# Attention with mixed heads, then two MoE layers, on one core: first loads on two DMA queues, the first block's scores moved in two halves, and a new layout of all steps

## The chip, the core and the metric

The kernel runs on one core of one Trainium2 chip. The core has five engines that run side by side, each working through its own instructions in order: TensorE (PE, whose weight loads are listed as PEld), VectorE (DVE), ScalarE (ACT), GpSimd (POOL) and SyncE (SP). SP computes nothing here; it issues the DMA transfers, which 16 DMA engines carry out. The metric is the device time of one execution in microseconds, as the median of several runs.

## What is computed

The reference has three stages, one after the other. The attention mixes the heads twice, before and after the softmax, so all 12 heads of a query are needed together.

```
scores = scale * q @ k^T                       # 4 batches, 12 heads, 448 queries, 448 keys, 64 wide
scores = einsum('bhij,hg->bgij', scores, w_pre)
attn   = exp(scores - max); attn /= sum + 1e-9
attn   = einsum('bhij,hg->bgij', attn, w_post)
x      = attn @ v                              # then (1792 tokens, 768)
x      = (s * relu(x @ w_in)**2 + b) @ w_out   # 768 -> 2048 -> 768
h      = x @ w_in2
out    = (h * cos(h)) @ w_out2
```

The second layer's weights arrive as float64 and are split on the chip into pairs of float32 parts. Most products are taken as a high and a low part (`qh`, `ql`; `wh`, `wl`; `gh`, `gl`) for precision.

## The kernel before

**Blocks and tiles.** The queries are cut into 16 blocks (`n`), four to a batch, of 120, 110, 110 and 110 queries. A block is worked on in tiles of R = 10 queries with all 12 heads, so that a tile has 120 rows and 448 columns; there are 180 tiles, and the first block has 12 of them. In this text they are counted from 0, so block 1 begins with tile 12 and block 4 with tile 45.

**Scores of a block.** `keys` and `queries` load and transpose k and q on PE (tiles `tk`, `tq`) and split them on ACT (`ks`, `qh`) and DVE (`ks`, `ql`). `scores` makes the product of one head with two matmuls (`sps`), copies it out on ACT or DVE (tile `s`; for block 0 a piece of the tile `at`), and then a DMA moves it into the block's tile `m`, where rows are ordered by query and head. This move (`m<-s`, in block 0 `m<-at`) is how the heads of one query come together. There are N_S = 4 buffers `s`, so a fifth copy waits until the move of the first has landed. There are two tiles `m`, so block n takes the one of block n-2.

**Work of a tile.** `shi` takes the high part of a tile's rows of `m` (tile `mh`, on ACT or POOL, line 421 or 423), POOL subtracts it (426), PE mixes the heads with three matmuls (tile `p`, 431 to 433), DVE takes the maximum (442), ACT the exponential with its sum (449), DVE makes the weights of a pair of tiles from the sums (`st`, 456 and 458; `w`, 462), PE mixes again and transposes (tile `a`, 471), and ACT or DVE keeps the result (`at`, 483 or 485). When two blocks are through, PE multiplies with v in three groups (`vps`, 506), the results are copied (`xo`) and stored to memory as `x`.

**The layers.** `mlp` loads x back, splits it (727), turns weights into pairs (673 to 701), and runs `hidden` (751) and `output` (814 and 842) for each of 16 weight pieces and four token groups.

**What sets the order.** No order is written out. Each step is given to a planner (class `Plan`) with a position, the engine or engines that may do it, a cost in ns, the steps it waits for, and the buffers that it takes and frees. The planner replays time with these costs: each time an engine is free, it gives it the ready step with the lowest position. It knows a fixed handover between engines (`SYNC`), a rate of transfers (`wire`), and the buffers' counts. The instructions are then written down in the order of that replay. On the chip the engines keep this order and wait by semaphores. So a cost in the planner moves nothing by itself, but it can change which step stands before which, and which of two engines gets a step. The constants `STEP`, `OFF`, `W1`, `W2`, `TOK` and the like only set positions. All transfers stand on SP's queue.

## Time and profile before

| | |
|---|---|
| median of three runs | 1465.22 us (1461.92 to 1465.97) |
| the profiled execution, its own time | 1466.36 us |
| its span, from first to last instruction | 1464.4 us, so 2.0 us lie around it |
| PE busy | 1411.6 us, 96% |
| DVE, ACT, POOL busy | 1202.2, 766.5, 622.2 us |
| mean granted clock of TensorE | 0.984 |

A share of busy time says how often an engine has something in it, over stages that differ: here the attention up to about 520 us, then the layers. What an engine waits for in a stretch is read from the idle time ahead of an instruction and the engine that ended it. The granted clock is given as a share of the full level (2.4 GHz); 0.5 is the lower level (1.2 GHz).

### The profile page before, as it was taken

The page shows a single profiled execution, that of the slowest core. Times are in us where ns is not written, and L with a number is a line of the kernel's source. Part 1 is how long each engine was busy: PE and PEld are TensorE (multiplying, and loading weights), DVE is VectorE, ACT ScalarE, POOL GpSimd, SP SyncE. Part 2 cuts the span into 40 slices and gives each one's busy share as a digit, 9 for nine tenths or more (in the row PEclk, how much of TensorE's full clock was granted, in tenths as well). Part 3 has the DMA queues.
Part 4 walks back from the last instruction along what each step waited for, and adds up shares of the span by engine and source line. Part 5 has one row for each costly group of instructions (what it writes and reads, how often), then busy time and mean ns, then how long its engine had stood idle before and what let it go on. Part 6 is the DMA issues. An engine that isn't in the chain of part 4 may idle for free.

```text
span 1464.4 us, 23087 instructions
## 1 busy us (share of the span) xinstructions
PE 1411.6 (96%) x8220; PEld 1228.8 (84%) x8220; DVE 1202.2 (82%) x2195; ACT 766.5 (52%) x1605; POOL 622.2 (42%) x554
## 2 busy tenths in 40 slices
PE   5898999999999799999999999999999999999998
PEld 4787888887888677888888888888999898998998
DVE  4687788677877779888987878798898999999975
ACT  4676676666767655433322332356655455454442
POOL 0554564445545535333432432424544454544431
PEclk8899999999999999999999999999999999999999
DMA  6645374464454352221212112111211211211103
GB/s 162 145 133 140 112 168 131 130 153 119 126 145 132 104 170 79 71 65 55 66 54 65 46 63 65 44 33 44 65 55 44 65 55 44 66 44 60 59 33 119
DMA packets 159485, 129.20 MB, mean 88 GB/s; under 512 B 93867, under 2 KB 147083, under 8 KB 159371
## 3 DMA queue, kind: packets, MB, share of 16 engines
q1 hardware_dynamic: 159371, 127.73, 31.0%
q8 instruction: 65, 1.06, 0.3%
q14 instruction: 49, 0.40, 0.1%
...
## 4 chain that ended last, share of the span: by engine, by line
PE 85%; DMA 6%; DVE 5%; ACT 2%; POOL 1%; issue 1%; SPq 1%; DVEq 0%; POOLq 0%; ACTq 0%
PE h L751 30%; PE o L842 16%; PE o L814 15%; PE a L471 8%; PE vps L506 5%; PE sps L357 4%; DMA m<-s 2%; PE p L431 2%; PE p L433 2%; PE p L432 2%; DMA qn<-in_q_dram 1%; PE tq L326 1%; DVE st L442 1%; DMA m<-x 1%; SPq L222 1%
## 5 line engine op out<-in xcount | busy, mean ns | idle before, releaser
L699 POOL TENSOR_TENSOR cm<-ca,wh 128x384 f32<-128x384 f32 x128 | 158.4, 1239 | 382.8 <-ACT wh L693 378.4
L426 POOL TENSOR_TENSOR m<-m,mh 120x448 fp32r<-120x448 f32 x180 | 208.2, 1162 | 189.0 <-ACT mh L421 176.1
L751 PE MATMUL h<-m,wh 128*128 128x512 f32 x672 | 215.7, 390 | 0.0
L471 PEld LDWEIGHTS a<-w,e 120*112 120x112 f32 x1440 | 172.8, 182 | 32.7 <-issue 13.4
L471 PE MATMUL a<-w,e 120*112 120x120 f32 x1440 | 181.5, 274 | 15.2 <-DVE w L462 14.7
L751 PE MATMUL h<-x,wh 128*128 128x256 f32 (+1 forms) x768 | 190.1, 338 | 1.1 <-DVE x L727 1.0
L701 POOL TENSOR_TENSOR wl<-cm,ce 128x384 fp32r<-128x384 f32 x128 | 148.3, 1160 | 83.2 <-DVE ce L697 79.2
L751 PE MATMUL h<-m,wl 128*128 128x512 f32 x384 | 150.3, 391 | 0.0
L751 PEld LDWEIGHTS h<-x,wh 128*128 128x128 f32 x768 | 131.7, 188 | 18.1 <-DVE x L727 2.3
L751 PEld LDWEIGHTS h<-m,wh 128*128 128x128 f32 x672 | 125.2, 188 | 25.6 <-issue 0.7
L814 PE MATMUL o<-gh,wl 128*128 128x512 f32 (+1 forms) x384 | 139.7, 364 | 0.8 <-POOL wl L701 0.8
L814 PE MATMUL o<-gl,wh 128*128 128x512 f32 (+1 forms) x384 | 139.6, 364 | 0.0
L814 PE MATMUL o<-gh,wh 128*128 128x512 f32 (+1 forms) x384 | 139.3, 363 | 0.0
L449 ACT ACTIVATE e<-p,st 120x448 f32<-120x448 f32 x180 | 114.1, 634 | 37.0 <-DVE st L442 34.6
L751 PE MATMUL h<-x,wl 128*128 128x512 f32 (+1 forms) x384 | 129.8, 338 | 0.0
L442 DVE TENSOR_REDUCE st<-p 120x1 f32<-120x448 f32 x180 | 109.9, 615 | 16.6 <-PE p L433 15.8
L791 POOL TENSOR_TENSOR tb<-ta,tb 128x512 f32<-128x512 f32 (+1 forms) x64 | 80.4, 1257 | 101.2 <-ACT tb L789 95.9
L842 PE MATMUL o<-wh,gl 128*128 128x384 f32 x448 | 114.0, 335 | 0.0
L842 PE MATMUL o<-wl,gh 128*128 128x384 f32 x448 | 113.9, 335 | 0.0
L842 PE MATMUL o<-wh,gh 128*128 128x384 f32 x448 | 113.8, 334 | 0.0
L675 DVE SCALAR_TENSOR_TENSOR cm<-cm,raw 128x384 f32<-128x384 f32 x128 | 95.7, 748 | 20.2 <-ACT cm L673 20.1
L851 DVE TENSOR_TENSOR acc<-acc,o 128x384 f32<-128x384 f32 x196 | 101.0, 544 | 13.1 <-PE o L842 13.0
...
## 6 DMA issues: line engine op xcount, KB each, us to landing
m<-s SPq DMA_DIRECT2D x144, 192.5 KB
raw<-in_moe_w_in_dram SPq DMA_DIRECT2D x64, 384.0 KB
raw<-in_moe_w_out_dram SPq DMA_DIRECT2D x64, 384.0 KB
...
m<-s SPq DMA_DIRECT2D x36, 210.0 KB
...
out_dram<-acc SPq DMA_DIRECT2D x14, 384.0 KB
...
```

The costliest lines, as they stand in the source:

```text
L426: a2 = pl.add(p - OFF[1] * STEP, "pool", 1110, lambda hh=hh, src=src: nc.gpsimd.tensor_tensor(out=src(), in0=src().bitcast(F32), in1=hh.ti ...
L442: nc.vector.tensor_reduce(out=hst.tile[:, 0, z:z + 1], in_=hp.tile, axis=AX, op=ALU.max, negate=True)
L449: nc.scalar.activation(out=he.tile, in_=hp.tile, func=AF.Exp, bias=hst.tile[:, 0, z:z + 1], accum_out=hst.tile[:, 1, z:z + 1])
L471: nc.tensor.matmul(out=ha.tile[:, c * L:(c + 1) * L], lhsT=he.tile[:, c * CH:(c + 1) * CH], rhs=hw2.tile[:, z], start=True, stop=True)
L675: a = pl.add(p0 + dp, "dve", 470, lambda hm=hm, high=high: nc.vector.scalar_tensor_tensor(out=hm.tile, in0=hm.tile, scalar=2.0 ** -15, in1 ...
L699: a = pl.add(p0 + 6 * dp, "pool", 1050, lambda hm=hm, ha=ha, flat=flat: nc.gpsimd.tensor_tensor(out=hm.tile, in0=ha.tile.bitcast(F32), in1 ...
L701: got.append(pl.add(p0 + 7 * dp, "pool", 1050, lambda hm=hm, he=he, flat=flat: nc.gpsimd.tensor_tensor(out=flat(1), in0=hm.tile, in1=he.ti ...
L751: nc.tensor.matmul(out=hp.tile, lhsT=w, rhs=cols(z_, j, k)[:, 0], start=(k == 0 and y == 0), stop=(k == KD - 1 and y == 2))
L791: a = pl.add(p + 7 * dp, "pool", n * 2.4 + 100, lambda h1=h1, h2=h2: nc.gpsimd.tensor_tensor(out=h2.tile, in0=h1.tile, in1=h2.tile, op=ALU ...
L814: nc.tensor.matmul(out=hp.tile, lhsT=w, rhs=x, start=(c == 0 and y == 0), stop=(c == 1 and y == 2))
L842: nc.tensor.matmul(out=hp[e].tile, lhsT=x, rhs=w[:, e * HD:(e + 1) * HD], start=(c == 0 and y == 0), stop=(c == 1 and y == 2))
L851: got.append(pl.add(p, "dve", 470, lambda e=e, hp=hp, view=view: nc.vector.tensor_tensor(out=view(), in0=view(), in1=hp[e].tile, op=ALU.ad ...
```

## The change

The first loads (k and q of block 0, the mask and the two mixing matrices) and the first half of each head's move in block 0 may now stand on SP's queue or on ACT's; the planner chooses. The three constants' loads get a low position (`CST`), so they come early. Block 0 loads each q once and not twice; POOL makes the second copy on the chip. In block 0 each head's move into `m` is split in two (`SUB`): queries 0 to 59 first, 60 to 119 with a higher position (`SECOND`), and a tile waits only for the half that it lies in. In block 0's keys the high part may be taken by DVE too. The planner gets other numbers: a handover for each engine, a dearer PE before 26 us (`COLD`), other costs of steps and of issues, a lower rate of transfers. All position constants are new. No instruction of the steady part is of a new kind.

```diff
-    SYNC = 130.0
+    SYNC = dict(pe=210.0, act=150.0, dve=130.0, pool=90.0, sp=130.0, none=130.0)
+    COLD = 26000.0
...
+                    elif e == "pe" and t < self.COLD:
+                        end = t + 1.8 * s["engs"][e]
...
-                        wire = max(end + 650.0, wire) + s["nbytes"] / 360.0
+                        wire = max(end + 650.0, wire) + s["nbytes"] / s["rate"]
...
-STEP = 2427.2
+STEP = 2364.9
...
+        if two:
+            return pl.add(pos, ("sp", "act"), (cost, cost), lambda e: (nc.sync if e == "sp" else nc.scalar).dma_start(out=out(), in_=in_()), after, take, use, nbytes=nbytes, behind=behind)
...
+    SUB = [2 if n == 0 else 1 for n in range(NBLK)]
...
-            e = pl.add(p + 500 + 100 * z, "act", 430.0, lambda z=z: hi(z), [a])
...
+            e = pl.add(p + 500 + 100 * z, ("act", "dve"), (480.0, 580.0), lambda e, z=z: hi(z, e), [a]) if not b else pl.add(p + 500 + 100 * z, "act", 480.0, lambda z=z: hi(z, "act"), [a])
...
-        for i in range(2):
...
+        for i in range(2 if n else 1):
...
+        if not n:
+            d.append(pl.add(p - 1000, "pool", 340.0, lambda: nc.gpsimd.tensor_scalar(out=raw()[:, :, 1], in0=raw()[:, :, 0], scalar1=1.0, scalar2=0.0, op0=ALU.mult, op1=ALU.add), d))
...
-            m_done.setdefault(n, []).append(dma(p + QZ * z + 1000, place, held, rows * S * 4, [e], use=[hs], behind=m_done.get(n, [])[:1]))
+            rs = rows // SUB[n]
+            for u in range(SUB[n]):
...
+                    return hm.tile.bitcast(F32).rearrange("(r h) t j -> r h t j", h=H)[:, h, u * rs // R:(u + 1) * rs // R]
...
+                    d = dma(p + u * SECOND, place, lambda: held()[u * rs:(u + 1) * rs], rs * S * 4, [e], use=[hs],
+                            behind=m_done.get(n, [])[:1] + (m_sub[n, 0] if u else []), cost=870.0, two=SUB[n] > 1 and u == 0)
...
-        a1 = pl.add(p - OFF[0] * STEP, e, (540.0, 480.0)[:len(e)], shi if len(e) > 1 else lambda shi=shi: shi("pool"), m_done[n], take=[hh])
+        a1 = pl.add(p - OFF[0] * STEP, e, (540.0, 480.0)[:len(e)], shi if len(e) > 1 else lambda shi=shi: shi("pool"), m_sub[n, t["t"] // (BLOCKS[n % 4][1] // R // SUB[n])], take=[hh])
...
-OFF = (4.214, 4.426, 3.27, 2.518, 2.539, 1.825)
-AVP = (2.733, 2696.6)
+OFF = (3.52, 4.361, 3.326, 2.518, 1.368, 2.311)
+AVP = (1.516, 1918.9)
...
+SECOND = 9999.326
+CST = -2999.464
...
-W1 = (-1.242, 4.431)
-W2 = (-1.044, 7.344)
+W1 = (-2.306, 4.548)
+W2 = (-3.818, 7.382)
```

The order of the instructions shows what becomes of this. On SP's queue, at the start of the program, these are the transfers of block 0 before (`at<-in_k` and `at<-in_q` are the loads, `m<-at` the moves of its scores, `qn` the queries of block 1, `w` the mixing matrices):

```order
L222 DMA ident<-in_cst_dram 128x128
L222 DMA at<-in_k_dram 112x4x64 x4
L222 DMA at<-in_q_dram 120x4x64 x2
L222 DMA at<-in_k_dram 112x4x64 x4
L222 DMA at<-in_q_dram 120x4x64 x2
L222 DMA at<-in_k_dram 112x4x64 x4
L222 DMA at<-in_q_dram 120x4x64 x2
L222 DMA m<-at 10x12x448 x4
L222 DMA mask<-in_cst_dram 120x10
L222 DMA m<-at 10x12x448 x3
L222 DMA qn<-in_q_dram 110x4x64 x2
L222 DMA w_110<-in_w_pre_dram 120x1x12
```

After these stand `w_post`, five more `m<-at`, four `qn` and four `m<-s`. Then come, before the last four `m<-s` of block 1, six more loads of q and v, four `m<-s`, two loads of v and four of the next batch's k. The same queue of the changed kernel:

```order
L228 DMA ident<-in_cst_dram 128x128
L227 DMA at<-in_k_dram 112x4x64 x3
L227 DMA at<-in_q_dram 120x4x64
L227 DMA at<-in_k_dram 112x4x64
L227 DMA w_110<-in_w_post_dram 120x1x12
L227 DMA at<-in_k_dram 112x4x64 x2
L227 DMA at<-in_q_dram 120x4x64
L227 DMA m<-at 10x6x448 x7
L228 DMA qn<-in_q_dram 110x4x64 x4
L228 DMA m<-at 10x6x448 x3
L228 DMA qn<-in_q_dram 110x4x64 x2
L228 DMA m<-at 10x6x448 x9
```

SP now has 9 loads ahead of the first move instead of 18 (both besides `ident`), 19 half moves instead of 12 whole ones, and after them the 12 moves of block 1 with only five loads of q between them; loads of v and of the next k come later.

On ACT's queue, at the start of the program, the changed kernel has this (before, ACT begins with the table load and issues nothing):

```order
L227 DMA mask<-in_cst_dram 120x10
L227 DMA at<-in_k_dram 112x4x64 x4
L227 DMA w_110<-in_w_pre_dram 120x1x12
L227 DMA at<-in_k_dram 112x4x64
L227 DMA at<-in_q_dram 120x4x64
L227 DMA at<-in_k_dram 112x4x64
L306 ACT_TABLE_LOAD
L306 ACTIVATE ks<-tk 64x448 x4
L343 ACTIVATE qh<-tq 128x480
L306 ACTIVATE ks<-tk 64x448 x4
L378 ACTIVATE at<-sps 120x448 x2
L227 DMA m<-at 10x6x448
```

Nine issues now stand ahead of the table load, and further on four more half moves each stand between two copies of scores.

On DVE, in the stretch in which the scores of block 4 are made (tiles 37 to 41 before), its copies `s<-sps` stand like this among the work of the tiles before the change:

```order
L368 COPY s<-sps 120x448 x2
L456 TENSOR_SCALAR st<-st 120x2
L442 TENSOR_REDUCE st<-p 120x1
L458 RECIPROCAL st<-st 120x2
L462 TENSOR_TENSOR w_1521<-wq,st 120x240
L333 TENSOR_TENSOR ql<-tq,qh 128x480
L302 TENSOR_TENSOR ks<-tk,ks 64x448 x2
L368 COPY s<-sps 120x448
L442 TENSOR_REDUCE st<-p 120x1
L368 COPY s<-sps 120x448
L456 TENSOR_SCALAR st<-st 120x2
L368 COPY s<-sps 120x448
```

and in the changed kernel:

```order
L380 COPY s<-sps 120x448
L345 TENSOR_TENSOR ql<-tq,qh 128x480
L312 TENSOR_TENSOR ks<-tk,ks 64x448 x2
L467 TENSOR_REDUCE st<-p 120x1 x2
L481 TENSOR_SCALAR st<-st 120x2
L510 COPY at<-a 112x48x10
L483 RECIPROCAL st<-st 120x2
L487 TENSOR_TENSOR w_1493<-wq,st 120x240
L312 TENSOR_TENSOR ks<-tk,ks 64x448 x2
L345 TENSOR_TENSOR ql<-tq,qh 128x480
L467 TENSOR_REDUCE st<-p 120x1 x2
L481 TENSOR_SCALAR st<-st 120x2
```

Five copies have become one. Over the whole program DVE's copies of scores go from 66 to 48 and ACT's from 114 to 132; DVE's copies `xo` from 42 to 2 and ACT's from 6 to 49 (rows of the order, where one row may be one half of a result); ACT's `mh` from 130 to 105 and POOL's from 50 to 75. On PE the 12 products of block 4 stood between the mixing of tiles 36 and 41, and now stand between those of tiles 34 and 41; blocks 6, 8, 10, 12 and 14 move in the same way. The three groups `vps` of blocks 12 and 13 move too: the last of them stood behind the mixing of tile 168 and now stands behind that of tile 166; no more of them follow until all tiles are mixed.

## Rows read from the trace of the kernel before

**Rows 1.** Windows of whole stages: us, busy of each engine, granted clock, DMA share

```profile
80.00:480.00 400.00, 384.04 (x2830) 327.84 (x2829) 305.73 (x627) 276.23 (x652) 198.29 (x194) 0.98 0.51 135
480.00:525.00 45.00, 34.74 (x257) 28.43 (x258) 38.29 (x75) 29.98 (x68) 22.50 (x18) 0.92 0.37 123
565.00:1452.00 887.00, 887.00 (x4584) 784.86 (x4583) 776.08 (x1345) 393.94 (x743) 356.98 (x301) 1.00 0.19 56
```

**Rows 2.** Timeline of SP's queue, the first 28 us: start, length, transfer

```profile
8.92 2.56 SPq L222 DMA_DIRECT2D at<-in_k_dram  x4
11.53 1.14 SPq L222 DMA_DIRECT2D at<-in_q_dram  x2
...
21.92 0.82 SPq L222 DMA_DIRECT2D w<-in_w_pre_dram  x1
...
23.69 4.25 SPq L222 DMA_DIRECT2D m<-at  x5
```

**Rows 3.** Windows of 10 us, the last three columns: granted clock, DMA share, GB/s

```profile
10.00:20.00 10.00, 8.50 (x37) 6.83 (x37) 7.36 (x12) 7.63 (x15) 0.00 (x0) 1.00 0.66 173
40.00:50.00 10.00, 9.95 (x68) 8.84 (x66) 8.68 (x20) 7.15 (x19) 6.83 (x7) 1.00 0.92 186
```

**Rows 4.** Timeline of ACT and POOL, start of the program to the first tile

```profile
0.73 1.28 ACT L298 ACT_TABLE_LOAD   x1 [0.73 <-PEq L904]
6.06 1.09 ACT L298 ACTIVATE ks<-tk 64x448 fp32r<-64x448 f32 x2 [4.04 <-PE tk L289]
...
23.76 0.54 ACT L366 ACTIVATE at<-sps 120x448 f32<-120x448 f32 x1 [0.83 <-PE sps L357]
33.04 0.58 ACT L421 ACTIVATE mh<-m 120x448 fp32r<-120x448 f32 x1 [1.15 <-DMA qn<-in_q_dram]
33.14 0.56 POOL L423 TENSOR_SCALAR mh<-m 120x448 fp32r<-120x448 f32 x1 [32.70 <-DMA qn<-in_q_dram]
```

**Rows 5.** Timeline of SP's queue, 46 to 58 us

```profile
47.92 6.25 SPq L222 DMA_DIRECT2D rk<-in_k_dram  x4
54.29 3.46 SPq L222 DMA_DIRECT2D m<-s  x4
```

**Rows 6.** Timeline of PE: first product of tile 12, and two later waits

```profile
62.85 0.46 PE L431 MATMUL p<-mh,wp_h 120*120 120x448 f32 x1 [2.06 <-ACT mh L421]
76.96 1.04 PE L471 MATMUL a<-w,e 120*112 120x120 f32 x8 [0.40 <-DVE w L462]
143.78 1.05 PE L471 MATMUL a<-w,e 120*112 120x120 f32 x8 [3.03 <-DVE w L462]
```

**Rows 7.** PE's waits, 64 to 480 us: total us, times, longest

```profile
PE a L471 <- DVE w L462: 10.1, 8, 3.0
PE p L431 <- ACT e L449: 4.0, 8, 1.1
```

**Rows 8.** Timelines of DVE and of ACT, 142 to 144 us

```profile
142.10 0.62 DVE L368 COPY s<-sps 120x448 f32<-120x448 f32 x1 [1.70 <-DMA m<-s]
143.29 0.54 ACT L366 ACTIVATE s<-sps 120x448 f32<-120x448 f32 x1 [4.14 <-DMA m<-s]
```

**Rows 9.** Windows behind three of the waits, columns as in rows 1

```profile
145.00:148.00 3.00, 2.96 (x13) 2.52 (x12) 1.91 (x6) 1.88 (x5) 0.47 (x1) 0.54 0.53 165
265.00:271.00 6.00, 5.66 (x25) 5.46 (x26) 3.39 (x9) 3.83 (x10) 1.13 (x1) 0.50 0.50 139
388.00:391.00 3.00, 3.00 (x14) 2.76 (x13) 1.69 (x5) 2.52 (x7) 2.27 (x2) 0.50 0.48 151
```

**Rows 10.** The end of the attention: a PE wait, and the window behind it

```profile
491.24 0.70 PE L431 MATMUL p<-mh,wp_h 120*120 120x448 f32 x1 [3.97 <-ACT e L449]
497.00:517.00 20.00, 14.79 (x105) 12.58 (x104) 19.11 (x36) 14.81 (x36) 12.77 (x10) 1.00 0.31 104
```

**Rows 11.** All waits of the program: ACT and DVE for a free `s`

```profile
ACT s L366 <- DMA m<-s: 17.6, 13, 4.1
DVE s L368 <- DMA m<-s: 11.4, 15, 1.7
```

More of the change, by code (lines that the diff above doesn't have):

```diff
@@ L52, in hold, with add @@
         return Hold(ring)
-    def add(self, pos, eng, cost, fn, after=(), take=(), use=(), lag=0.0, behind=(), nbytes=0, port=False):
+    def add(self, pos, eng, cost, fn, after=(), take=(), use=(), lag=0.0, behind=(), nbytes=0, port=False, rate=200.0):
         n = len(self.steps)
@@ L63, in add @@
         self.steps.append(dict(id=n, pos=pos, engs=dict(zip(engs, costs)), fn=fn, after=[a for a in after if a is not None],
-                               take=take, use=use, lag=lag, behind=list(behind), nbytes=nbytes, port=port))
+                               take=take, use=use, lag=lag, behind=list(behind), nbytes=nbytes, port=port, rate=rate))
         return n
@@ L219, in attention, with dma @@
         pl.ring(name, cap, name != "ps")
-    def dma(pos, out, in_, nbytes, after=(), take=(), use=(), behind=()):
-        return pl.add(pos, "sp", 515.0 if not use else 700.0, lambda: nc.sync.dma_start(out=out(), in_=in_()), after, take, use, nbytes=nbytes, behind=behind)
+    def dma(pos, out, in_, nbytes, after=(), take=(), use=(), behind=(), cost=650.0, two=False):
+        if two:
+            return pl.add(pos, ("sp", "act"), (cost, cost), lambda e: (nc.sync if e == "sp" else nc.scalar).dma_start(out=out(), in_=in_()), after, take, use, nbytes=nbytes, behind=behind)
+        return pl.add(pos, "sp", cost, lambda: nc.sync.dma_start(out=out(), in_=in_()), after, take, use, nbytes=nbytes, behind=behind)
     tiles, first = [], []
+    SUB = [2 if n == 0 else 1 for n in range(NBLK)]
     for n in range(NBLK):
@@ L240, in attention @@
     wq = one.tile([L, H, R], F32, name="wq")
-    d_id = dma(-5200, lambda: ident, lambda: cst[:, 0:128], 65536)
-    d_mk = dma(5000, lambda: mask, lambda: cst[0:L, 128:128 + R], 4800)
-    d_w = [dma(5000, lambda i=i: w12[:, i], lambda w=w: w.rearrange("(o h) g -> o h g", o=1).to_broadcast([R, H, H]), 5760) for i, w in enumerate((w_pre, w_post))]
+    d_id = dma(-5200, lambda: ident, lambda: cst[:, 0:128], 65536, cost=450.0)
+    d_mk = dma(CST, lambda: mask, lambda: cst[0:L, 128:128 + R], 4800, two=True)
+    d_w = [dma(CST, lambda i=i: w12[:, i], lambda w=w: w.rearrange("(o h) g -> o h g", o=1).to_broadcast([R, H, H]), 5760, cost=950.0, two=True) for i, w in enumerate((w_pre, w_post))]
     hw = pl.hold("e")
@@ L261, in attention @@
     KW = 8 * D
[L262 removed]
+    mh, m_first, m_done, m_sub, later = {}, {}, {}, {}, []
     m_all = m_p.tile([128, 2, 12 * S], F32R, name="m")
@@ L281, in keys @@
             d.append(dma(p - 6000, lambda h=h: load(h), lambda h=h: k[b, 2 * g + h].rearrange("(p z) d -> p z d", z=4), CH * KW * 2,
-                         take=[hr] if b and h == 0 else [], behind=d if h else m_done[0][-1:] if b else [s_open]))
+                         take=[hr] if b and h == 0 else [], behind=d if h else m_done[0][-1:] if b else [s_open], two=not b))
         bank, ring, tag = (ps_s, "ps", "s") if b else (ps_a, "pa", "a") if g % 2 else (ps_p, "pp", "p")
@@ L318, in queries @@
         d = []
-        for i in range(2):
-            d.append(dma(p - 8000 if n else p - 5500, lambda i=i: load(i), lambda: q[b, 4 * g:4 * g + 4, i0:i0 + rows, :].rearrange("h i d -> i h d"), rows * 2048,
-                         take=[hr] if n and i == 0 else [], behind=d if i else m_done[0][5:6] if n else [s_open]))
+        for i in range(2 if n else 1):
+            d.append(dma(p - 8000 if n else p - 5500, lambda i=i: load(i), lambda: q[b, 4 * g:4 * g + 4, i0:i0 + rows, :].rearrange("h i d -> i h d"), rows * 1024,
+                         take=[hr] if n and i == 0 else [], behind=d if i else m_done[0][-1:] if n else [s_open], two=not n, cost=600.0))
+        if not n:
+            d.append(pl.add(p - 1000, "pool", 340.0, lambda: nc.gpsimd.tensor_scalar(out=raw()[:, :, 1], in0=raw()[:, :, 0], scalar1=1.0, scalar2=0.0, op0=ALU.mult, op1=ALU.add), d))
         def trans():
@@ L381, in attention @@
         scores(0, g, PRO[0] * g + PRO[2])
+    for move in later:
+        move()
     for n in range(1, NBLK):
@@ L507, in prod, with evac @@
                                              start=(c == 0), stop=(c == 3), tile_position=(0, 64 * y))
-            a = pl.add(p + AVP[1] * 2 * pp, "pe", 2 * AVC - 150, prod, kept[b, hf] + [d for c in range(4) for d in v_done[b, c]],
+            a = pl.add(p + AVP[1] * 2 * pp, "pe", 3300.0, prod, kept[b, hf] + [d for c in range(4) for d in v_done[b, c]],
                        take=[hp], use=[hb] + [vh[b, c] for c in range(4)])
-            def evac(e, hp=hp, ho=ho, blocks=blocks, base=base, wid=wid):
+            def evac(e, hp=hp, ho=ho, blocks=[(i0 + u * rows // SUB[4 * b + 2 * hf + z], rows // SUB[4 * b + 2 * hf + z]) for z, (i0, rows) in enumerate(blocks)
+                                              for u in range(SUB[4 * b + 2 * hf + z])], base=base, wid=wid):
                 ho.tile = xo_p.tile([128, 2 * width[0]], F32, tag="xo", name="xo")[:, :2 * wid].rearrange("p (g n) -> p g n", g=2)
@@ L627, in dma @@
     def dma(pos, out, in_, nbytes, after=(), take=(), use=(), behind=()):
-        return pl.add(pos, "sp", 515.0 if not use else 700.0, lambda: nc.sync.dma_start(out=out(), in_=in_()), after, take, use, nbytes=nbytes, behind=behind)
+        return pl.add(pos, "sp", 450.0, lambda: nc.sync.dma_start(out=out(), in_=in_()), after, take, use, nbytes=nbytes, behind=behind, rate=300.0)
     c_sb = [dma(t_start - 15000, lambda i=i: P["sc"][:, i:i + 1], lambda a=a: a.rearrange("(a o) -> a o", a=1).to_broadcast([128, 1]), 512, [g_right]) for i, a in enumerate((s, b))]
```

51 lines of the change are left out of this document (30 added, 21 removed).

## The prediction

> **What bounds the kernel now.** First I read the windows of whole stages [rows 1]. From 565 to 1452 us PE is busy for all of 887 us at the full clock: the layers are bound by PE. The change leaves the number of PE's matmuls as it is, so this stretch should keep its length, whatever the new positions do to DVE or POOL there. What can be won lies before 565 us. From 80 to 480 us PE is idle for 400 - 384.0 = 16.0 us and runs at a mean of 0.98 of the clock; from 480 to 525 us it is idle for 10.3 us; the rest is in the first 65 us.
>
> Then I read the start in order of time. SP issues the 18 loads of k and q without a gap until 12.67 us, at 2.56/4 = 0.64 us for a k and 1.14/2 = 0.57 us for a q [rows 2]. The DMA engines are then busy for 0.66 of the time, while later they reach 0.92 [rows 3]. So the first loads are held by the issuing queue, not by the engines. The last score of block 0 is copied by 23.76 + 0.54 = 24.30 us [rows 4]; but SP spends 21.92 to 23.69 us on the two mixing matrices and then 4.25 us on the last five moves, until 27.94 us [rows 2]. The first tile's `mh` starts at 33.04 us [rows 4], 5.10 us behind the end of that last issue. POOL had been idle for 32.70 us. Tile 12, the first of block 1, is mixed at 62.85 us after another wait of 2.06 us [rows 6]: between block 1's moves SP issued four loads of the next k for 6.25 us, and its last four moves only from 54.29 to 57.75 us [rows 5].
>
> Last the middle. PE's waits from 64 to 480 us sum to 14 us, 10.1 of them for the weights `w` from DVE and 4.0 for the exponential [rows 7]. Neither engine is short of time there (DVE 305.7, ACT 276.2 of 400 us) [rows 1]. At 143.78 us PE waits for 3.03 us [rows 6], and just before, DVE stood 1.70 us and ACT 4.14 us in front of a copy into `s` whose buffer was still being moved [rows 8]. An engine works in order, so maximum, weights and exponential stood behind that copy. This is block 4, whose 12 scores stand within five tiles. Block 2, whose 12 stand within eight, shows a wait of 0.40 us [rows 6]. In all, ACT waits 17.6 us and DVE 11.4 us for a free `s` [rows 11].
>
> **The change part by part.** I cost it against the profiled execution: 1464.4 us of span and 2.0 around it, 1466.36 us. The median of the runs is 1465.22, 1.1 us less.
>
> *Start.* On two queues SP has 9 loads and `ident`, ACT nine. By the rows SP needs 6 x 0.64 + 2 x 0.57 + 0.8 + 0.4 = 6.2 us and is free near 7 us instead of 12.7. What an issue costs on ACT no row shows; I take SP's, which gives 6 x 0.64 + 0.57 + 0.8 + about 0.5 = 5.7 us, so ACT ends near 6.4 us and, since the table load of 1.28 us now stands behind, can begin at 7.7 instead of 6.06 us [rows 4]. That loss is partly covered by DVE, which takes the first key. Nothing covers the rest: until the last score ACT has 9 + 3 + 8 + 1 activations at about 0.54 us and five half moves. A half move has no row; its ends are 0.43 us (half of 4.25/5 = 0.85) and 0.85 us, and I take 0.85, the row of the same transfer, because the loads show no saving with size either (0.64 for 112 KB, 0.57 for 120 KB). So ACT needs 11.3 + 4.3 = 15.6 us and ends near 23.3 us: the last copy is hardly earlier than 24.30. The gain comes behind it: no matrices and no row of five whole moves are left, the last half is issued by about 24.2 us instead of 27.9, and lands 5.1 us later at most and 2.6 us (half the bytes) at least. The first `mh` then starts at 27 to 29 us, 4 to 6 us earlier.
>
> POOL's three copies of q are bounded by nothing below and by 0.56 us each above (the row of 448 columns [rows 4]; these have 256); POOL is idle there, but each lies between its q and the transpose. They replace three loads of 0.57 us and 120 KB.
>
> Tile 12 checks this from SP's side: from 24.4 us on SP still has, until the last move of block 1, six q (3.4 us), 12 second halves (10.2), 12 moves of block 1 (10.2) and five q (2.9), and ends at 51.1 us instead of 57.75. With halves at 0.43 it would be 46, and PE's own work would then be what ends last. **Start: -6 us, bounds -2 to -9.** What is late next is the second half of block 0 (tile 6), with PE doing `a` and block 1's scores meanwhile.
>
> *Middle.* Blocks 4, 6, 8, 10, 12 and 14 now spread their scores over seven tiles, and of block 4's 12 copies DVE keeps one where it had five between the same weights. If all six cost what block 2 does, 14.1 - 6 x 0.4 = 11.7 us of waits go. With them go the stretches at the lower level (1.2 GHz) that followed three of the waits, 12 us in which PE was busy for 11.6 [rows 9]; at the higher level half of that would do, 5.8 us. What speaks against taking it all: the copies that leave DVE go to ACT, where the exponential stands behind them. I take half of 17.5. **Middle: -9 us, bounds 0 to -17.**
>
> *End of the attention.* PE waits 3.97 us at 491 us, and DVE is busy for 19.1 of 20 us behind that [rows 10]. By the order, DVE's steps for the layers among the last 13 tiles fall from about 16 to 8; the rest comes after, beside 3.1 us of `a` and three `vps`. Against this, the last `vps` that could fill a gap now comes two tiles earlier. **End: -2 us, bounds -7 to +4.**
>
> *Layers.* **0**: PE is the bound, and the steps that moved lie beside it [rows 1].
>
> Sum: 1466.36 - 6 - 9 - 2 = 1449.4, or 1448.2 against the median; I say 1449.
>
> **Rivals.**
>
> *Only the start gains.* The waits of the middle move from DVE to ACT and stay as long. For it: 17.6 of the 29.0 us of waits for `s` are ACT's already [rows 11]. Against: eight tiles instead of five did away with them in block 2. Time 1465.2 - 6 = 1459, at most 1461.
>
> *Two queues bring nothing at the start.* The same DMA engines carry both queues; if these set the pace, issuing earlier only makes the transfers queue. 1,704 KB of loads and 1,260 KB of half moves (by the shapes in the order, 4 bytes each) at the 186 GB/s of the busiest row take 16 us [rows 3], less than the 24 us that the copies need, so the row speaks against it; block 1's moves could still meet it. Then only the middle and the end are left: 1465.2 - 11 = 1454. The Trainium skill's page "DMA: Bandwidth & Descriptors", section "Issuing engines are not separate DMA queues", says so for the general case: issuing from several engines saves only the sequencer's time to initiate, since all run on the same 16 DMA engines; by that rule alone the start would give nothing. The trace agrees with half of it: here it is the sequencer's time that is short, with the engines at 0.66.
>
> *Slower: ACT blocks.* ACT now makes nearly all copies of `s` in the even blocks, and each waits for a move; the exponential of the next tile stands behind it, then `w`, then `a` on PE. If all 29.0 us that ACT and DVE wait now came together on ACT and reached PE, the middle would lose 29.0 - 14.1 = 15 us more: 1465.2 - 6 + 15 = 1474. It decides from the point where more than 14.1 + 6 = 20 us of such waits reach PE. Against: with seven tiles a copy has half as much again of the time it had.
>
> *Nothing to measure.* The parts cancel: a start of -2 and a middle of 0: 1463.
>
> **How the numbers follow.** The forecast (1442 to 1457) 0.57, only the start 0.17, two queues without gain 0.08, ACT blocks 0.10, nothing 0.08. A change of 0.3% (4.4 us) is about what a measurement of this kernel can tell from none. Faster: 0.57 + 0.08 + 0.13 of the second case = 0.78. Same: 0.08 + 0.04 = 0.12. Slower: 0.10. The range leaves out the slower case and the best corner of the bounds: 1439 to 1463; the forecast's own is 1442 to 1457.
>
> **What would show it.** Right: SP's last first load ends near 7 us; ACT's first activation near 7.7; the first `mh` at 27 to 29 us and tile 12's product near 57; no wait of PE over 1 us between 64 and 480 us, none for `w` behind a copy into `s`; granted clock above 0.984. Wrong: ACT's issues last over 1 us each; waits of `e` on ACT and of `s` on the moves grow beyond 20 us; the end from tile 167 to 179 grows; PE falls idle after 565 us. A time near 1459 would say that the middle kept its waits; one above 1466, that ACT's queue became the bound.

## The result, and the profile after

The changed kernel takes 1447.99 us (median of 4 runs, 1446.86 to 1451.16), the kernel before on the same chip 1465.6 us (4 runs); the ratio is 0.9888, 95% interval 0.9865 to 0.9911. The profiled execution took 1446.86 us, with a span of 1445.0 us and a mean granted clock of 0.992 (before 1464.4 and 0.984). The forecast was 1449. The sum is right; of its three terms the start failed, and the middle came in part from something that the sum had no term for, as the runs below show. The two traces lie 19.4 us apart and the medians 17.6; the places named below add up to the 19.4.

First the windows of whole stages after, columns as in [rows 1]:

```profile
80.00:480.00 400.00, 388.37 (x2917) 333.16 (x2915) 287.80 (x589) 306.19 (x724) 217.66 (x221) 1.00 0.55 143
480.00:525.00 45.00, 38.59 (x243) 30.70 (x243) 34.41 (x68) 26.13 (x57) 18.46 (x16) 0.92 0.47 149
565.00:1433.00 868.00, 868.00 (x4484) 768.86 (x4483) 749.54 (x1317) 379.20 (x717) 346.68 (x293) 1.00 0.19 56
```

The layers are PE's as before. From 80 to 480 us PE has 11.6 us of idle time instead of 16.0, and its mean clock is 1.00 instead of 0.98; DVE is 17.9 us less busy and ACT 30.0 us more.

To place the gain I use the start of a tile's first mixing product (L431 before, L456 after). Tiles 0, 12, 20, 167 and 179 start at 34.83, 62.85, 82.27, 477.46 and 510.17 us before, at 31.69, 64.72, 78.06, 460.88 and 487.35 us after. So the change gains 3.1 us at tile 0, has lost 1.9 at tile 12, is 4.2 ahead at tile 20, gains 12.4 more until tile 167 (382.8 instead of 395.2 us), 6.2 more until tile 179, and gives 3.4 back behind it (957.65 instead of 954.2 us to the end). Other work of PE stands in another order around tiles 6 to 19, so tile 12 is a worse mark than tile 20.

Part of this is the clock. Before, PE runs at the lower level (1.2 GHz) for much of the time from 62 to 72 us, behind its wait ahead of tile 12 [rows 6], and behind three waits of the middle [rows 9]; after, it does not. First the kernel before, then the changed one (the column behind the five engines is the granted clock):

```profile
62.00:72.00 10.00, 8.66 (x37) 7.59 (x38) 5.72 (x12) 6.32 (x15) 6.00 (x6) 0.66 0.29 77
```

```profile
62.00:72.00 10.00, 9.64 (x61) 7.68 (x60) 6.70 (x13) 6.99 (x17) 7.90 (x8) 1.00 0.94 182
```

PE's 8.66 busy us at 0.66 would be some 3 us less at the full level (an estimate): most of the 4.2 us at tile 20.

The start after, on ACT's queue and ACT, on SP's queue, and on PE (three timelines):

```profile
4.86 0.90 ACTq L227 DMA_DIRECT2D w<-in_w_pre_dram  x1
6.69 0.61 ACTq L227 DMA_DIRECT2D at<-in_k_dram  x1
7.78 0.36 ACTq L227 DMA_DIRECT2D at<-in_q_dram  x1
8.55 0.60 ACTq L227 DMA_DIRECT2D at<-in_k_dram  x1
9.19 1.28 ACT L306 ACT_TABLE_LOAD   x1 [9.19 <-DMA w<-in_w_pre_dram]
10.48 2.20 ACT L306 ACTIVATE ks<-tk 64x448 fp32r<-64x448 f32 x4
...
24.73 0.76 ACTq L227 DMA_DIRECT2D m<-at  x1
25.54 0.54 ACT L378 ACTIVATE at<-sps 120x448 f32<-120x448 f32 x1 [0.84 <-ACT at L378]
26.11 0.77 ACTq L227 DMA_DIRECT2D m<-at  x1
31.06 0.58 ACT L446 ACTIVATE mh<-m 120x448 fp32r<-120x448 f32 x1 [4.98 <-DMA qn<-in_q_dram]
```

```profile
7.16 1.58 SPq L227 DMA_DIRECT2D at<-in_k_dram  x2
9.20 0.34 SPq L227 DMA_DIRECT2D at<-in_q_dram  x1
15.96 9.46 SPq L227 DMA_DIRECT2D m<-at  x7
25.47 3.15 SPq L228 DMA_DIRECT2D qn<-in_q_dram  x4
```

```profile
30.54 0.97 PE L338 MATMUL tq<-ident,qn 110*128 110x110 f32 x4 [6.01 <-DMA qn<-in_q_dram]
31.69 0.73 PE L456 MATMUL p<-mh,wp_h 120*120 120x448 f32 x1 [0.19 <-DMA m<-at]
...
47.99 1.87 PE L496 MATMUL a<-w,e 120*112 120x120 f32 x16 [2.48 <-DVE w L487]
49.61 0.44 PE L456 MATMUL p<-mh,wp_h 120*120 120x448 f32 x1
```

To be read here: the later issues on both queues do not follow each other; ACT's seventh stands 0.93 us behind its sixth. ACT loads its table only at 9.19 us and copies the first key at 10.48 us, not at 7.7. Its last half moves alternate with its last copies of scores, so the last copy ends at 26.08 us, against 24.30 before [rows 4], and the last half is issued by 26.88. The first `mh` stands 4.2 us behind the end of that issue. The load of block 1's queries, issued from 25.47 us, holds PE for 6.01 us ahead of tile 0, until 30.54; the first `mh` starts only half a microsecond later.

PE's waits from 64 to 480 us (columns as in [rows 7]), then ACT's and DVE's for a free `s` (as in [rows 11]):

```profile
PE p L456 <- ACT e L474: 4.5, 7, 1.7
PE a L496 <- DVE at L510: 3.0, 4, 0.8
PE a L496 <- DVE w L487: 2.5, 4, 1.0
```

```profile
ACT s L378 <- DMA m<-s: 5.7, 7, 1.6
...
DVE s L380 <- DMA m<-s: 2.9, 6, 1.4
```

PE's 10.1 us for `w` have become 2.5, and the 29.0 us for `s` 8.6.

### The profile page after: what moved, and what is told of

Its sections match the earlier page's. It is cut to its first block, busy times and chain, and to the rows that moved or that the text cites. A ratio compares the mean times of both kernels' runs of the same rounds, so it can differ in the third digit from the quotient of the medians.

```text
span 1445.0 us, 23109 instructions
## 1 busy us (share of the span) xinstructions
PE 1401.5 (97%) x8220; PEld 1222.4 (85%) x8220; DVE 1160.9 (80%) x2132; ACT 780.2 (54%) x1646; POOL 637.6 (44%) x582
## 4 chain that ended last, share of the span: by engine, by line
PE 90%; DVE 4%; DMA 3%; ACT 2%; issue 1%; POOL 0%; SPq 0%; ACTq 0%; DVEq 0%; POOLq 0%
PE h L779 32%; PE o L870 16%; PE o L842 16%; PE a L496 9%; PE vps L531 5%; PE sps L369 4%; PE p L456 2%; PE p L458 2%; PE p L457 2%; PE tq L338 1%; DMA m<-s 1%; DVE ks L312 1%; DMA qn<-in_q_dram 1%; DVE st L467 1%; ACT e L474 1%
## 5 line engine op out<-in xcount | busy, mean ns | idle before, releaser
L727 POOL TENSOR_TENSOR cm<-ca,wh 128x384 f32<-128x384 f32 x128 | 163.4, 1279 | 364.0 <-ACT wh L721 364.0
L496 PEld LDWEIGHTS a<-w,e 120*112 120x112 f32 x1440 | 167.7, 178 | 28.5 <-issue 5.3
L496 PE MATMUL a<-w,e 120*112 120x120 f32 x1440 | 176.2, 270 | 12.7 <-DVE w L487 9.4
L729 POOL TENSOR_TENSOR wl<-cm,ce 128x384 fp32r<-128x384 f32 x128 | 144.6, 1131 | 85.4 <-DVE ce L725 80.2
L474 ACT ACTIVATE e<-p,st 120x448 f32<-120x448 f32 x180 | 113.7, 632 | 25.6 <-DVE st L467 23.6
L849 DVE TENSOR_TENSOR acc<-acc,o 128x512 f32<-128x512 f32 (+1 forms) x168 | 101.3, 615 | 11.9 <-PE o L842 11.2
```

Source lines behind the costliest of these rows:

```text
L474: nc.scalar.activation(out=he.tile, in_=hp.tile, func=AF.Exp, bias=hst.tile[:, 0, z:z + 1], accum_out=hst.tile[:, 1, z:z + 1])
L496: nc.tensor.matmul(out=ha.tile[:, c * L:(c + 1) * L], lhsT=he.tile[:, c * CH:(c + 1) * CH], rhs=hw2.tile[:, z], start=True, stop=True)
L727: a = pl.add(p0 + 6 * dp, "pool", 1050, lambda hm=hm, ha=ha, flat=flat: nc.gpsimd.tensor_tensor(out=hm.tile, in0=ha.tile.bitcast(F32), in1 ...
L729: got.append(pl.add(p0 + 7 * dp, "pool", 1050, lambda hm=hm, he=he, flat=flat: nc.gpsimd.tensor_tensor(out=flat(1), in0=hm.tile, in1=he.ti ...
L849: a = pl.add(p, "dve", n * 1.05 + 66, lambda hp=hp, view=view: nc.vector.tensor_tensor(out=view(), in0=view(), in1=hp.tile, op=ALU.add), [ ...
```

## The experiments

Twelve kernels ran, each timed in turn with the kernel before. Each has its ratio and interval. e5 to e8 ran on another chip than the other eight, so rows of the table are compared by their ratios. For the place of a gain I read the same tiles as above. Executions differ a little even with one order: e1 to e4 keep the changed kernel's order, and from tile 20 to tile 167 they take 382.4 to 384.5 us, so 2 us between two traces are no finding there; at tile 20, e1 to e3 lie between 77.09 and 80.46 us.

| kernel | median us | ratio (95%) | tile 0 | tile 12 | tile 20 | 20 to 167 | 167 to 179 |
|---|---|---|---|---|---|---|---|
| before (profiled: 1466.36) | 1465.6 | 1 | 34.83 | 62.85 | 82.27 | 395.2 | 32.7 |
| after | 1447.99 | 0.9888 (0.9865-0.9911) | 31.69 | 64.72 | 78.06 | 382.8 | 26.5 |
| e1 one queue | 1447.86 | 0.9887 (0.9866-0.9909) | 31.45 | 65.93 | 78.55 | 383.2 | 26.0 |
| e2 table first | 1446.66 | 0.9880 (0.9851-0.9910) | 32.34 | 65.08 | 80.46 | 384.5 | 25.4 |
| e3 loads on SP | 1447.24 | 0.9883 (0.9861-0.9904) | 31.93 | 64.60 | 77.09 | 382.4 | 25.8 |
| e4 whole moves | 1451.54 | 0.9907 (0.9883-0.9932) | 34.48 | 66.75 | 80.10 | 382.8 | 26.4 |
| e5 before, new spread | 1459.81 | 0.9979 (0.9960-0.9998) | 33.96 | 60.09 | 76.76 | 393.8 | 33.2 |
| e6 before, all numbers | 1454.36 | 0.9937 (0.9921-0.9953) | 34.43 | 65.09 | 80.17 | 386.8 | 31.4 |
| e7 after, old spread | 1456.1 | 0.9943 (0.9925-0.9961) | 32.17 | 65.79 | 79.79 | 385.3 | 26.3 |
| e8 copies by turns | 1453.21 | 0.9925 (0.9908-0.9943) | 32.22 | 66.21 | 80.61 | 385.7 | 24.9 |
| e9 before, transfers' numbers | 1456.47 | 0.9946 (0.9926-0.9966) | 36.36 | 64.03 | 78.00 | 388.8 | 33.7 |
| e10 before, engines' numbers | 1463.38 | 0.9993 (0.9981-1.0006) | 35.13 | 60.85 | 77.72 | 397.1 | 33.4 |
| e11 before, numbers and spread | 1449.47 | 0.9892 (0.9872-0.9913) | 33.84 | 64.00 | 77.99 | 378.9 | 34.0 |
| e12 queries at the sixth move | 1447.40 | 0.9889 (0.9869-0.9910) | 34.49 | 62.28 | 77.05 | 381.0 | 25.6 |

### The start: e1 to e4

e1 puts, where the planned order is written out, all that chose between the queues on SP:

```diff
+                if st[i]["engs"].keys() == {"sp", "act"}:
+                    e = "sp"
```

> The changed kernel with its order kept; the loads and half moves that chose between SP and ACT all go to SP. Theory A (ACT's own issuing cost the start its gain: from its fifth issue on each stands until an earlier transfer of the program has landed, so the table load went from 0.73 to 9.19 us and the first copy of a key from 6.06 to 10.48): the first copy is back at 6 to 7 us, SP issues the loads until 11 to 13 us, the first mh starts at 29 to 31 us instead of 31.06, tile 12 is mixed at 60 to 63 us instead of 64.72; the time is 2 to 4 us below the changed kernel's 1448. Theory B (the loads arrive no sooner and no later with either queue, the rest of the start binds): tile 12 within 1 us of 64.72, time 1447 to 1449. Theory C (the second queue did help, and something else took it back): tile 12 at 67 us or later, time 1450 or more.

Theory B's figures hold, but for 0.2 us at tile 12 (65.93); the time is the changed kernel's. ACT loads its table early and copies the first key 2.6 us sooner (not 3.5 to 4.5, as theory A had it); of that 0.2 us is left at tile 0 (lines of ACT, SP and PE):

```profile
0.73 1.28 ACT L308 ACT_TABLE_LOAD   x1 [0.73 <-PEq L934]
7.89 1.09 ACT L308 ACTIVATE ks<-tk 64x448 fp32r<-64x448 f32 x2 [5.87 <-PE tk L298]
...
29.31 0.58 ACT L448 ACTIVATE mh<-m 120x448 fp32r<-120x448 f32 x1 [5.29 <-DMA qn<-in_q_dram]
```

```profile
15.79 11.05 SPq L229 DMA_DIRECT2D m<-at  x12
26.89 2.31 SPq L230 DMA_DIRECT2D qn<-in_q_dram  x4
```

```profile
30.81 0.97 PE L340 MATMUL tq<-ident,qn 110*128 110x110 f32 x4 [7.36 <-DMA qn<-in_q_dram]
```

What takes it back stands further on. The last first half is issued by 26.84 us here, the last of twelve on SP, and by 26.88 in the changed kernel. The first `mh` does start at 29.31 us instead of 31.06. But in PE's order a transpose of block 1's queries stands ahead of tile 0, and their loads, issued behind that half, hold PE until 30.81 us (30.54 in the changed kernel).

e2 lets ACT load its table before it issues:

```diff
+    warm = one.tile([1, 2], F32, name="warm")
+    nc.vector.memset(warm, 0.0)
+    nc.scalar.activation(out=warm, in_=warm, func=AF.Copy)
```

> The changed kernel with a 2-element fill and activation written first, so that ACT loads its table before its issues and not behind them. Theory A (ACT's late start is what the first tiles feel): the first copy of a key starts 1.0 to 1.3 us earlier (9.2 to 9.5 us instead of 10.48), first mh and tile 12 also about 1 us earlier, time 1446.5 to 1447.5. Theory B (the key's landing or the rest binds): the copy starts earlier by less than 0.4 us or the gain is gone by tile 12; time 1448.

Theory B: the first copy starts at 10.55 us. The table load is done early, but the issues that stand ahead of the copy now end at 10.50 us instead of 9.16; why they do is not shown. The time, 1446.66, lies in theory A's range, but its interval holds both. e3 puts the loads alone on SP:

```diff
+                if st[i]["engs"].keys() == {"sp", "act"} and not st[i]["after"]:
+                    e = "sp"
```

> The changed kernel with the first loads on SP alone and the half moves still on both queues: tells whether the loads or the half moves on ACT cost more. Theory A: as with all on SP for the first copy of a key (6 to 7 us); the five half moves on ACT take some 3 to 5 us of ACT's time but spare SP as much, so tile 12 is mixed at 60 to 63 us, time 1444 to 1446. Theory B: tile 12 within 1 us of 64.72, time 1447 to 1449. If this one is better than all on SP by 1 us or more at tile 12, the half moves on ACT are the good part of the second queue; if worse, none of it is.

Theory B's figures hold again. At tile 12 e3 is 1.3 us ahead of e1, which by the expectation would make the half moves the good part of the second queue; it is less than the 2 us by which traces can differ, and the times are alike. So neither the loads nor the half moves on ACT's queue bring or cost anything that can be measured in the time. What becomes of the loads is read from the windows from 4 to 8 and 8 to 12 us (last columns: DMA share, GB/s); first the kernel before, then the changed one, then e3, both of these up to 16 us:

```profile
4.00:8.00 4.00, 2.13 (x9) 1.52 (x10) 0.79 (x2) 1.48 (x3) 0.00 (x0) 1.00 0.83 187
8.00:12.00 4.00, 3.13 (x14) 2.61 (x14) 3.56 (x6) 2.83 (x6) 0.00 (x0) 1.00 0.81 184
```

```profile
4.00:8.00 4.00, 2.19 (x9) 1.53 (x10) 1.96 (x4) 0.00 (x0) 0.00 (x0) 1.00 1.03 199
8.00:12.00 4.00, 3.30 (x16) 2.58 (x15) 0.93 (x2) 2.76 (x4) 0.81 (x2) 1.00 0.93 179
12.00:16.00 4.00, 2.48 (x6) 1.80 (x7) 3.87 (x7) 3.89 (x9) 0.41 (x1) 1.00 0.00 0
```

```profile
4.00:8.00 4.00, 1.93 (x8) 1.32 (x8) 1.43 (x3) 0.00 (x0) 0.00 (x0) 1.00 0.75 169
8.00:12.00 4.00, 2.67 (x13) 2.12 (x12) 3.65 (x7) 3.55 (x7) 0.40 (x1) 1.00 0.50 108
12.00:16.00 4.00, 3.13 (x11) 2.73 (x12) 2.78 (x5) 2.28 (x5) 0.81 (x2) 1.00 0.58 131
```

The kernel before has 18 loads of k and q and the changed one 15, so the second queue is judged against e3, which has the same loads on one queue. With two queues the engines are full (1.03 of the time) and move 199 instead of 169 GB/s, then 179 instead of 108; from 12 us on nothing is left to load, where e3 still moves 131 GB/s. So the loads do arrive sooner, and theory B's reason is wrong where its figures hold. They bring nothing in the end: ACT stands in its issues meanwhile and copies the first key at 10.48 us (8.07 in e3), and ahead of tile 0 stand block 1's queries, whose loads come behind the last first half on one queue as on two (e1). The Trainium skill says on the page "DMA: Bandwidth & Descriptors", section "Issuing engines are not separate DMA queues", that transfers from all issuing engines run on the same 16 DMA engines, and that issuing from several saves only the time of issuing. The trace agrees: the last load is issued by 9.54 us instead of 13.38 (e1), and the rate rises until the engines are full.

e4 keeps the order but moves block 0's scores whole, in the first halves' places. Its tiles of block 0 hold their query rows in another order than the steps behind them take, so these rows of the output change places; the amount of work is that of the changed kernel, less twelve moves.

```diff
+                if st[i]["engs"].keys() == {"sp"} and "skip" in st[i]:
+                    continue
...
+                    if u:
+                        pl.steps[d]["skip"] = True
```

> The changed kernel with block 0's scores moved whole at the place of the first halves; the second halves' steps issue nothing. Twelve issues of about 0.8 us leave SP before block 1's moves. If the halves are what gave the first tile 3.1 us (34.83 to 31.69), tile 0 goes back by 1 to 4 us (33 to 36 us) while tile 6 is no longer late (45 to 47 us instead of 49.61), and tile 12 is mixed 1 to 4 us earlier than 64.72: the halves cost the start more than they give, time 1444 to 1447. If the halves pay, tile 12 is mixed at 65 us or later and the time is 1448 or more.

The halves pay, by the expectation's figures (66.75 us at tile 12, 1451.54 in all), and clearly at tile 0, which goes back 2.8 us where e1 to e3 differ by 0.9. Tiles 12 and 20 come 2.0 us later, which is no more than the 2 us by which traces can differ, and the intervals of e4 and of the changed kernel overlap, so what is left of it in the time is not shown. That twelve issues leave SP helps nobody: tile 6 comes at 51.63 us, later still.

### The middle: e5 to e8

e5 and e7 exchange only the two pairs that spread the even blocks' scores, e5 into the kernel before and e7 back out of the changed one:

```diff
-W1 = (-1.242, 4.431)
-W2 = (-1.044, 7.344)
+W1 = (-2.306, 4.548)
+W2 = (-3.818, 7.382)
```

> The kernel before with only the two pairs of numbers that place the even blocks' scores taken from the change (scores over seven tiles; queues, halves, costs and all other positions as before). From tile 12 to tile 167 before needs 477.46 - 62.85 = 414.6 us, the changed kernel 396.2. Theory P (the prediction's: spreading the scores removes the waits behind copies into s, and the slow clock behind them): tile 12 to 167 takes 398 to 406 us, ACT's and DVE's waits for s fall from 29.0 us to under 10, time 1449 to 1457. Theory R (the spread alone gives little; the middle came from the planner's numbers, by which copies left DVE, and from the other positions): 411 to 417 us, time 1461 to 1467.

> The changed kernel with only the two pairs of numbers that place the even blocks' scores put back (scores in five tiles again). Theory P: ACT's and DVE's waits for s come back (15 us or more instead of 5.7), PE's waits in the middle rise by 6 to 12 us, tile 12 to 167 takes 404 to 412 us instead of 396.2, time 1456 to 1464. Theory R: under 400 us, time 1448 to 1452.

The spread alone gives 3 us in time (0.9979), nearly theory R's; from tile 20 to 167 it gains 1.4 us, and 12 to 167 takes 410.5 us, between the two. Its waits, PE's from 64 to 480 us and those for a free `s`:

```profile
PE p L431 <- ACT e L449: 7.7, 7, 3.4
PE a L471 <- DVE w L462: 5.9, 8, 1.2
```

```profile
ACT s L366 <- DMA m<-s: 10.1, 14, 2.5
DVE s L368 <- DMA m<-s: 3.9, 7, 0.8
```

Here the waits for `s` do fall, from 29.0 to 14.0 us, and PE's waits for `w` from 10.1 to 5.9; but PE's waits for the exponential on ACT rise from 4.0 to 7.7, and its idle time from 80 to 480 us does not fall (18.6 us against 16.0).

Taken back out of the changed kernel the spread costs 8 us in the median, at the low edge of theory P, but its trace (an execution of 1452.92 us) loses only 2.5 us between tiles 20 and 167, 12 to 167 takes 399.3 us as theory R said, and the waits for `s` stay at 8.5 us. Put on top of the planner's numbers (e11 below, against e6) it gains 7.9 us between tiles 20 and 167, and some 6.6 in time by the ratios. So the spread is worth 3 to 8 us, least when it stands alone, and in the changed kernel not through the waits for `s` that the prediction named.

e6 gives the kernel before the planner's numbers alone (its edit is that of e9 and e10 together):

> The kernel before with only the planner's numbers of the change (durations, wait costs by engine, rates and bytes of transfers); positions, one queue and whole moves as before. Theory P: the positions are old, scores stay clumped, waits for s stay above 15 us and tile 12 to 167 takes 409 to 418 us (before 414.6), time 1460 to 1468. Theory R: the planner knows the engines better, so fewer steps stand in front of PE: 398 to 407 us, time 1450 to 1458. It may also come out slower (1470 or more), since the old positions were fitted to the old numbers: then the numbers alone are no gain.

12 to 167 takes 401.9 us and the time is 1454.36: theory R. DVE makes 79 copies of `s` and 44 of `xo` there, before 66 and 42, so it is not by taking copies off DVE that the numbers gain. e8 checks that from the other side:

```diff
+                if st[i]["engs"] == {"act": 430.0, "dve": 535.0}:
+                    turn += 1
+                    if turn > 12:
+                        e = "act" if turn % 2 else "dve"
```

> The changed kernel with its order kept; from block 1 on, the copies of scores into s go by turns to ACT and DVE (ACT has most of them in the change). Theory P (DVE, with maximum and weights behind such a copy, is the engine that must not stand): DVE's waits for s come back, PE's waits for w rise, tile 12 to 167 takes 400 to 406 us instead of 396.2, time 1452 to 1458. Theory S (with scores over seven tiles it does not matter which engine copies): 395 to 398 us, time 1447 to 1450.

12 to 167 takes 400.1 us and the time is 5 us above the changed kernel's, at the low edge of theory P (the two intervals just overlap); but from 20 to 167 only 2.9 us are lost, and the waits for `w` from 64 to 460 us are 4.2 us instead of 1.0. Which engine copies matters by a few us at most.

### Which numbers: e9 and e10; what is left: e11 and e12

e9 takes the transfers' numbers:

```diff
-                        wire = max(end + 650.0, wire) + s["nbytes"] / 360.0
+                        wire = max(end + 650.0, wire) + s["nbytes"] / (200.0 if s["id"] < self.n_att else 300.0)
...
-        return pl.add(pos, "sp", 515.0 if not use else 700.0, lambda: ...
+        return pl.add(pos, "sp", 650.0 if not use else 870.0, lambda: ...
```

> The kernel before with only the planner's numbers of transfers taken from the change: issue costs 0.65 and 0.87 us instead of 0.515 and 0.70, 200 and 300 bytes/ns instead of 360, the true bytes of q and v. With all the planner's numbers the same kernel took 386.8 us from tile 20 to tile 167 (before 395.2, the changed kernel 382.8). Theory D (the old plan put copies into s in front of a buffer whose move it thought done; with the true rates the copies come later and nobody stands in them): 386 to 389 us, ACT's and DVE's waits for s from 64 to 460 us fall from 25.1 us to 12 or less, time 1454 to 1457. Theory E (the waits between engines are what the plan had wrong): 393 to 396 us, time 1462 to 1466.

e10 takes the engines' numbers:

```diff
-    SYNC = 130.0
+    SYNC = dict(pe=210.0, act=150.0, dve=130.0, pool=90.0, sp=130.0, none=130.0)
+    COLD = 26000.0
```

> The kernel before with only the planner's numbers of the engines taken from the change: the wait after a step by engine (0.09 to 0.21 us, and 0.06 more in front of PE) instead of 0.13 for all, PE at 1.8 times its durations in the first 26 us, keys' copies 0.05 and 0.06 us dearer, the product with v 0.05 us cheaper. Theory D: tile 20 to 167 within 2 us of 395.2, waits for s stay above 18 us, time 1462 to 1467. Theory E: 386 to 390 us, time 1454 to 1458. If neither this one nor the one with the transfers' numbers has the gain alone, the two act together.

Theory D holds in both, in every figure. All waits of the program for a free `s`, and the windows from 80 to 480 us; first e9, then e10:

```profile
ACT s L366 <- DMA m<-s: 4.9, 6, 1.8
DVE s L368 <- DMA m<-s: 5.5, 6, 1.4
80.00:480.00 400.00, 384.86 (x2870) 324.21 (x2868) 318.24 (x656) 275.50 (x648) 193.35 (x186) 1.00 0.53 140
```

```profile
ACT s L369 <- DMA m<-s: 17.9, 12, 3.3
DVE s L371 <- DMA m<-s: 10.3, 9, 2.5
80.00:480.00 400.00, 379.49 (x2822) 322.45 (x2824) 306.68 (x629) 272.40 (x643) 192.13 (x187) 0.99 0.51 135
```

With the transfers' numbers the waits for `s` fall from 29.0 to 10.4 us, the middle runs at the full clock, and 8.4 us are gained in time; with the engines' numbers 28.2 us of them stay and nothing is gained. PE's idle time from 80 to 480 us is 15.1 us in e9 and was 16.0 before, so what e9 gains there is nearly all clock: the stretches at the lower level that followed the long waits [rows 9] are gone. The rows of before point to the rate: the transfers ran at 173 to 186 GB/s [rows 3], where the old plan reckoned with 360 bytes/ns and the new one with 200. By the old figure a move counts as done too soon, and the next copies are put in front of a full buffer. For q and v the old plan counted twice the bytes, which made up for the rate; for the moves and for k nothing did. e9 changes the costs of issues and the byte counts with the rate, so that it is the rate among the three is argued, not shown.

e11 has the edits of e6 and e5 together, and neither a second queue nor halves, doubling or new positions:

> The kernel before with all the planner's numbers and the two pairs that place the even blocks' scores; one queue, whole moves, both copies of q loaded, all other positions as before: what the change has without the parts that its first loads and first block bring. If the two act each for itself: about 1464 - 9 - 4 = 1451 by the times, tile 20 to 167 at 384 to 386 us, time 1449 to 1453, and what is left to the changed kernel's 1448 is the end of the attention (26.5 us from tile 167 to 179 there, 32.7 before, 31.4 with the numbers). If it reaches 1448 or less, two queues, halves and doubling give nothing; if it stays at 1454 or more, they or the other positions carry some 6 us.

1449.47 us, with an interval that is nearly the changed kernel's. It is at 77.99 us at tile 20, where the changed kernel is at 78.06, and it needs 3.9 us less until tile 167. Its 378.9 us are also less than the 384 to 386 expected of numbers and spread each for itself: they do more together. What the changed kernel has over it is the end of the attention, 26.5 instead of 34.0 us. All kernels with the new positions take 24.9 to 26.5 us there, all with the old 31.4 to 34.0: that gain goes with the positions. In the time, what two queues, halves, doubling and new positions together bring over e11 cannot be told from nothing (0.9888 against 0.9892).

e12 releases block 1's queries earlier:

```diff
-behind=d if i else m_done[0][-1:] if n else [s_open]
+behind=d if i else m_done[0][5:6] if n else [s_open]
```

> The changed kernel with block 1's queries released by block 0's sixth first move, as before, instead of its last. In the changed kernel PE stands 6.01 us in front of these queries' transposes until 30.54, because their loads were issued only at 25.47. Theory F (this wait is where the start's gain went): the wait falls under 3 us, PE makes four or five of block 1's scores before tile 0, tile 0 stays at 31 to 34 us, and from tile 20 on everything is 2 to 5 us earlier than in the changed kernel, time 1443 to 1446. Theory G (the half moves come later by as much as the queries come sooner, since they share the queue): tile 0 at 34 us or later, tile 20 within 1.5 us of 78.06, time 1447 to 1450.

Theory G. Its PE and ACT's queue:

```profile
27.99 0.97 PE L338 MATMUL tq<-ident,qn 110*128 110x110 f32 x4 [3.27 <-DMA qn<-in_q_dram]
30.19 0.97 PE L338 MATMUL tq<-ident,qn 110*128 110x110 f32 x4 [1.23 <-DMA qn<-in_q_dram]
...
34.49 0.37 PE L456 MATMUL p<-mh,wp_h 120*120 120x448 f32 x1
```

```profile
23.53 5.77 ACTq L227 DMA_DIRECT2D m<-at  x4
29.34 0.54 ACT L343 ACTIVATE qh<-tq 128x440 fp32r<-128x440 f32 x1 [5.84 <-DMA m<-at]
```

The queries' loads push the half moves back: ACT needs 5.77 us for four issues, tile 0 comes 2.8 us later, and tile 20 only 1.0 us earlier. Its profiled execution is the shortest seen (1440.66), its median no better than the changed kernel's. No kernel run here is measurably faster than the changed one; e11's middle with the new positions' end was not tried.

## Why the prediction came out right in sum and wrong in its terms

The terms were 6 + 9 + 2 = 17 us; by the marks in the traces they came out at 4.2 + 12.4 + 2.8 = 19.4. The forecast had too much for the start and too little for the middle; that the two nearly cancel is luck.

**Start (-6): this step failed.** "SP ... is free near 7 us" and "the last half is issued by about 24.2 us" overlooked two things. From their sixth issue on both queues stood until earlier transfers had landed; SP's last first load is issued by 9.54 us. And ACT, which issues and copies in turn, ended its last copy 1.8 us later than before, not earlier. The half's landing, taken up to the first `mh`, was within the bounds (4.2 us), its issue cost near the one chosen (0.77 us for half the bytes, against 0.85 for the whole). So the first `mh` came at 31.06 instead of 27 to 29. Tile 12 came at 64.72 instead of near 57: SP's sum of issues took no account of the waits for copies between them, and the last move of block 1 is issued by 58.89 us instead of 51.1. The 4.2 us at tile 20 are there with one queue too (e1, e3), and in e5, e9, e10 and e11, which have neither halves nor a second queue. e10 is at 77.72 us there and takes as long as the kernel before, so this mark says little of the time: some 3 us of it, by the estimate above, are the clock in the one trace of before. The rival "two queues bring nothing at the start" was right on the outcome and half right on the cause: the engines were full from 4 to 8 us, but the loads still ended sooner. It got 0.08 because I set 186 GB/s against 24 us of copies and not against the loads' own 12 us, and because the 0.66 that spoke against it is of 10 to 20 us, where loads are issued only until 12.67 us; from 4 to 8 and 8 to 12 us the kernel before already has 0.83 and 0.81.

**Middle (-9): right place, half the cause, too small.** The waits for `w` behind copies into `s`, and the lower level behind them, did go: 12.4 us from tile 20 (18.5 from tile 12, beyond the bound of 17). But the step "If all six cost what block 2 does" gave all of them to the spread, which carries 1.4 us of it in the traces alone, 2.5 when it is taken out of the changed kernel, and 7.9 on top of the numbers. The transfers' numbers carry 6.4 alone, all numbers 8.4, and numbers and spread together 16.3 (e11). For the numbers the sum had no term: I had read the rate in the diff and 173 to 186 GB/s in the rows and did not put the one beside the other.

**End (-2): 6.2 gained, 3.4 given back.** The net 2.8 is near the term; the gain until tile 179 is at the edge of the bound of 7. Of the return, 0.9 us is PE's wait for the first layer's `x` (1.7 us at 526.62, where before has 0.8). The clock covers the rest: a stretch at the lower level lies ahead of tile 179 before (510.17 us) and behind it after (487.35), so it is part of the gain until tile 179 and of the return. After, PE's 6.13 busy us at 0.50 would be some 3 us less at the full level (an estimate). First before, then after:

```profile
490.00:497.00 7.00, 5.44 (x22) 4.74 (x23) 4.90 (x12) 5.56 (x15) 3.81 (x3) 0.51 0.10 34
```

```profile
494.50:501.30 6.80, 6.13 (x35) 4.42 (x35) 4.85 (x11) 3.00 (x6) 3.70 (x3) 0.50 0.19 58
```

**Layers (0)**: right; 868 of 868 us busy. **ACT blocks**: fell; ACT's waits for `s` went down to 5.7 us. In e5, the spread without the numbers, PE's waits for ACT's exponential did grow as it had it, but the kernel did not become slower. **Only the start gains** fell the other way round: only the middle and the end did.

## What to carry to other kernels

Where a planner lays out the steps, first compare its durations and rates with the trace: a transfer that it thinks twice as fast as it is puts copies in front of full buffers, and the new spread alone gained little here (e5). A second issuing queue brings the loads in sooner only while the DMA engines have room, and that is worth something only if the second engine has nothing else to do and the next step hangs on the loads; check all three in the window where the transfers lie. When a change comes in a bundle, its most visible part need not be the one that pays: undo each alone, and build the rest without it.

## What the runs showed beyond that

An issue can stand like any instruction and hold its engine. The program's transfers share eight completion semaphores in turn over both queues, so a transfer's issue waits until the transfer that had its semaphore last has landed. In the changed kernel the fifth issue on ACT waits for the semaphore of ACT's first, the sixth for that of its second, and so on. The greatest sum of SP's waits of this kind in the first 12 us (total us, times, longest); two more make 0.8 us, and the kernel before has none:

```profile
SPq L227 <- DMA at<-in_k_dram: 1.7, 3, 0.9
```

On one queue such waits stayed hidden, since the loads were issued no faster than they landed (0.64 us each [rows 2]); on two they cost ACT its start (9.19 us to the table load) and, in e12, 5.77 us for four issues that take 0.77 us each when nothing is waited for.
